# Four accumulator banks shared between two users, and a new order of units, in an attention and bilinear-FFN kernel

## Chip, cores, metric

One core of a Trainium2 chip. The metric is the device time of one execution in microseconds (us), the median of several; the profiled span is about 1.5 to 2 us shorter.

Engines: PE is TensorE (matmuls), DVE is VectorE, ACT is ScalarE, POOL is GpSimd (here it issues the loads), SP is SyncE (it issues the stores).

## The reference

```python
# 8 batches, 8 heads, 576 positions, 64 per head, 32 memory slots
a = softmax(phi, over positions)
k_m, v_m = einsum('bhsm,bhsd->bhmd', a, k), einsum('bhsm,bhsd->bhmd', a, v)
attn = softmax(q @ k_m.T / 8) @ v_m          # (b,h,s,d)
x = attn as 4608 rows of 512
out = ((x @ w_a) * (x @ w_b)) @ w_out        # d_ff = 1536
```

The kernel never forms `x`. It folds `v_m` into `w_a` and `w_b` for each batch ("fold", `pva`, result `vab`), then multiplies the attention weights by the folded matrices ("up": `pa`, `pb`; their product is `ht`), then by `w_out` ("down": `po`, 12 matmuls for 128 rows of the result).

## The kernel before

A batch's attention is cut into units: exponentials (`exp`), sums over positions (`kv`, `pkv`), transposes (`kvt`, `qt`), scores (`sc`), denominators (`dn`, `pD`, then two reciprocals `rD`), normalise (`nr`, `pR`) and six folds (`va`). The order in which they are emitted is the order on every engine.

```python
    ps_up = tile_pool(bufs=2, PSUM)     # two names, pa and pb: four banks
    ps_dn = tile_pool(bufs=2, PSUM)     # po
    ps_at = tile_pool(bufs=2, PSUM)     # everything of attention, tag "at"
    ...
        def denominators():
            pD = ps_at.tile([P, HALF], F32, name="pD", tag="at")
            ... four matmuls into pD ...
            for z in range(2):
                nc.vector.reciprocal(out=t["rD"][:, sl], in_=pD[:, sl])
        def fold(n, z):
            pvas = [ps_at.tile([P, 512], F32, name="pva", tag="at") for _ in range(2)]
            ... eight matmuls, alternating between the two ...
            nc.scalar.copy(out=vabs[b][z][:, 0, sl], in_=pvas[0])
            nc.vector.tensor_copy(out=vabs[b][z][:, 1, sl], in_=pvas[1])
    ...
    # ups(steps, side, rate): up steps of two slots each; side units spread evenly
    # over the slots; rate downs per step. run(b, names): units with nothing beside.
    run(0, "exp0 exp1 kv0 kv1 kvt qt0 qt1 sc0 sc1 dn va0a va0b nr0 nr1")
    ups(steps(0, 0, 4))
    load(2)
    run(1, "exp0 exp1 kv0 kv1 kvt qt0 qt1 va0a va0b sc0 sc1")
    run(0, "va1a va1b")
    run(1, "dn")
    ups(steps(0, 4, 6), named(1, "- - nr0 nr1"))
    ups(steps(1, 0, 4) + steps(0, 6, 8), named(1, "va1a va1b"))
    run(0, "va2a va2b")
    ups(steps(1, 4, 8) + steps(0, 8, 12), ...)
    load(3)
    ups(steps(1, 8, 12), ..., 5.2)
    run(2, "dn va1a va1b nr0 nr1 va2a va2b")
    for b in range(2, B):
        ups(steps(b, 0, NFF), named(b + 1, every), 5.2)
```

Loads are issued in the order batch 0, a third of `w_a` and `w_b`, batch 1, the rest of the weights.

The softmax here doesn't subtract the row's maximum and nothing guards it: scores larger than these inputs give would overflow.

## Time and profile before

| | before |
|---|---|
| time, median of 4 runs (range) | 302.44 us (301.09 to 302.77) |
| span of the profiled run | 301.0 us |
| PE, DVE, ACT busy | 258.1, 185.2, 127.9 us |
| mean granted PE clock | 0.966 |
| first up matmul | 28.24 us |
| batch 2's ups start, downs done by then | 96.11 us, 20 |

"Busy" adds up durations of matmuls that overlap, so 86% busy does not mean that 14% could be won.

### The profile page before, as it was taken

What the parts mean: (1) busy time and instruction counts of PE and PEld (TensorE: products, weight loads), DVE (VectorE), ACT (ScalarE), POOL (GpSimd) and SP (SyncE); (2) the same over time, 40 slices, a digit from 0 to 9 for tenths busy, and PEclk for the clock granted to TensorE, in tenths of its full rate; (3) what the DMA queues carried; (4) which work ended last, traced back from release to release, by engine and by line L of the source; (5) the groups of instructions that cost most, each with busy time, mean ns of one, the idle gap of its engine ahead of it and who ended that gap; (6) DMA issues with size and microseconds to landing.
All of it is one profiled execution on the core that took longest, in us unless ns stands there. A gap on an engine that the chain in (4) does not pass through costs nothing.

```text
span 301.0 us, 6648 instructions
## 1 busy us (share of the span) xinstructions
PE 258.1 (86%) x2640; PEld 137.8 (46%) x2640; DVE 185.2 (62%) x382; ACT 127.9 (43%) x307; POOL 32.8 (11%) x53
## 2 busy tenths in 40 slices
PE   0255848879957999999999999899999999999993
PEld 0122514546522554455445554455445544566541
DVE  5055556777865485866678576758677567745410
ACT  3022434566443346352644446444644354433400
POOL 8522221001200120002000200000000000000000
PEclk9999975999995899999999999999999999999999
DMA  6999999991970399228930594122111111212234
GB/s 145 203 246 207 206 207 248 246 181 29 195 130 2 85 164 180 48 55 173 208 70 12 148 206 100 38 57 50 38 35 35 39 39 34 65 40 58 50 79 96
DMA packets 24367, 33.46 MB, mean 111 GB/s; under 512 B 1808, under 2 KB 18704, under 8 KB 24336
## 3 DMA queue, kind: packets, MB, share of 16 engines
q0 software_dynamic: 18576, 23.60, 42.9%
q1 hardware_dynamic: 5760, 9.44, 12.8%
q8 instruction: 20, 0.33, 0.4%
q14 instruction: 11, 0.09, 0.1%
HBM read 42.47 MB, written 9.44 MB: 172 GB/s over the span
## 4 chain that ended last, share of the span: by engine, by line
PE 81%; DVE 9%; DMA 3%; ACT 3%; issue 1%; POOL 1%; DVEq 0%; POOLq 0%
PE po L279 30%; PE pa L328 17%; PE pb L337 17%; PE pva L243 7%; DVE rD L222 4%; DMA kv_sb<-in_v_dram 3%; PE pkv L157 3%; PE pscore L199 3%; ACT vab L251 2%; PE pR L229 2%; DVE qT L148 1%; DVE A L231 1%; PE pT L178 1%; PE pD L216 1%; DVE ht L340 1%
## 5 line engine op out<-in xcount | busy, mean ns | idle before, releaser
L279 PE MATMUL po<-wo_sb,ht 128*128 128x512 f16 x432 | 118.0, 382 | 0.0
L340 DVE TENSOR_TENSOR ht<-a_sb,pb 128x288 f16<-128x288 f16 x192 | 78.4, 448 | 58.1 <-PE pb L337 51.2
L331 ACT CAST a_sb<-pa 128x288 f16<-128x288 f32 x192 | 68.0, 405 | 74.7 <-PE pa L328 73.6
L328 PE MATMUL pa<-A,vab 128*128 128x288 f16 x384 | 66.5, 295 | 0.9 <-DVE A L231 0.8
L337 PE MATMUL pb<-A,vab 128*128 128x288 f16 x384 | 65.6, 292 | 0.1
L279 PEld LDWEIGHTS <-ht 128*128 128x128 f16 x432 | 42.6, 99 | 24.4 <-issue 0.6
L251 ACT CAST vab<-pva 128x512 f16<-128x512 f32 x48 | 28.1, 585 | 50.0 <-PE pva L243 50.0
L337 PEld LDWEIGHTS <-vab 128*128 128x128 f16 x384 | 36.8, 100 | 25.7 <-issue 5.5
L328 PEld LDWEIGHTS <-vab 128*128 128x128 f16 x384 | 33.9, 100 | 24.1 <-issue 10.2
L252 DVE CAST vab<-pva 128x512 f16<-128x512 f32 x48 | 33.0, 688 | 17.1 <-PE pva L243 17.0
L243 PEld LDWEIGHTS <-kvT 64*32 64x32 f16 x384 | 7.4, 90 | 36.7 <-issue 26.1
L208 ACT ACTIVATE E<-pscore,rphi 128x288 f16<-128x288 f32 x32 | 14.3, 497 | 20.6 <-PE pscore L199 20.6
L148 DVE STREAM_TRANSPOSE qT<-q_sb 128x576 f16<-128x576 f16 x32 | 22.6, 748 | 0.0
L243 PE MATMUL pva<-wb_sb,kvT 64*32 64x512 f16 x192 | 14.2, 421 | 9.1 <-ACT vab L251 4.2
L157 PE MATMUL pkv<-kv_sb,exp_sb 64*32 64x192 f16 x576 | 9.6, 259 | 14.1 <-DMA kv_sb<-in_v_dram 13.2
L285 DVE TENSOR_SCALAR o_sb<-po 128x512 f32<-128x512 f32 x18 | 12.3, 683 | 14.9 <-PE po L279 14.9
L287 ACT ACTIVATE o_sb<-po 128x512 f32<-128x512 f32 x18 | 10.8, 599 | 16.9 <-PE po L279 16.8
L222 DVE RECIPROCAL rD<-pD 128x144 f16<-128x144 f32 x16 | 15.7, 1026 | 3.3 <-PE pD L216 3.2
L243 PE MATMUL pva<-wa_sb,kvT 64*32 64x512 f16 x192 | 12.6, 413 | 5.3 <-DVE rD L222 3.3
L231 DVE SCALAR_TENSOR_TENSOR A<-E,rphi,pR 128x288 f16<-128x288 f16 x32 | 14.9, 510 | 3.3 <-PE pR L229 2.6
L79 POOL DMA_DIRECT2D phi_sb<-in_phi_dram x8 | 6.2, 776 | 92.6 <-ACT exp_sb L138 64.8
L157 PEld LDWEIGHTS <-exp_sb 64*32 64x32 f16 x576 | 6.4, 96 | 19.2 <-issue 16.2
(33 smaller groups left out, 92.9 us busy)
## 6 DMA issues: line engine op xcount, KB each, us to landing
out_dram<-o_sb SPq DMA_DIRECT2D x72, 128.0 KB, 2.4
phi_sb<-in_phi_dram POOLq DMA_DIRECT2D x8, 576.0 KB, 5.3
kv_sb<-in_k_dram POOLq DMA_DIRECT2D x8, 576.0 KB, 7.7
kv_sb<-in_v_dram POOLq DMA_DIRECT2D x8, 576.0 KB, 9.8
q_sb<-in_q_dram POOLq DMA_DIRECT2D x8, 576.0 KB, 10.4
wa_sb<-in_moe_w_a_dram POOLq DMA_DIRECT2D x3, 512.0 KB, 19.8
wb_sb<-in_moe_w_b_dram POOLq DMA_DIRECT2D x3, 512.0 KB, 19.8
wo_sb<-in_moe_w_out_dram POOLq DMA_DIRECT2D x3, 512.0 KB, 20.7
```

What stands on the lines that cost most here:

```text
L148: nc.vector.transpose(out=t["qT"][:, hp, :], in_=qs[b][:, hp, :])
L157: nc.tensor.matmul(t["pkv"][g][32 * j:32 * j + 32, :], t["exp"][64 * r:64 * r + 64, hp, i, :], kvs[b][64 * r:64 * r + 64, :, hp, D * i:D * ...
L222: nc.vector.reciprocal(out=t["rD"][:, sl], in_=pD[:, sl])
L231: nc.vector.scalar_tensor_tensor(out=attn[b][:, g, sl], in0=t["E"][:, g, sl], scalar=t["rphi"][:, g:g + 1], in1=pR, op0=ALU.mult, op1=ALU. ...
L243: nc.tensor.matmul(pvas[g][32 * j:32 * j + 32, :], t["kvT"][64 * r:64 * r + 64, 4 + g, M * j:M * j + M], w_sbs[z][64 * r:64 * r + 64, hp, sl],
L251: nc.scalar.copy(out=vabs[b][z][:, 0, sl], in_=pvas[0])
L252: nc.vector.tensor_copy(out=vabs[b][z][:, 1, sl], in_=pvas[1])
L279: nc.tensor.matmul(po, ht[:, i, P * c:P * (c + 1)], wo_sb[:, i, :], start=(i == 0), stop=(i == NFF - 1))
L328: nc.tensor.matmul(pa, vab[0][:, g, fs], A[:, g, HALF * hf:HALF * (hf + 1)], start=(g == 0), stop=(g == 1))
L331: nc.scalar.copy(out=a_sb, in_=pa)
L337: nc.tensor.matmul(pb, vab[1][:, g, fs], A[:, g, HALF * hf:HALF * (hf + 1)], start=(g == 0), stop=(g == 1))
L340: nc.vector.tensor_tensor(out=ht[:, i, t0:t0 + HALF], in0=a_sbs[hf], in1=pb, op=ALU.mult)
```

## The change

The intent: let down and attention draw from one pool of four banks, each time the one unused for longest; give each up slot at most one unit of attention, with downs in every slot; run batch 0 alone up to its last up step, so that batch 1's loads can come last; keep the array clock up with products of zeros while the first inputs arrive. All evictions of the result go to ScalarE. `...` marks cuts, some runs of lines are abridged, and most comments are mine.

```diff
-    ps_dn = ...tile_pool(name="ps_dn", bufs=2, PSUM)
-    ps_at = ...tile_pool(name="ps_at", bufs=2, PSUM)
+    ps_any = ...tile_pool(name="ps_any", bufs=1, PSUM)      # tags bank0..bank3
...
+    class Banks:
+        def take(self, shape, dtype, name, hold=False):
+            n = next(x for x in self.order if x not in self.held)
+            self.order.remove(n); self.order.append(n)
+            if hold: self.held.add(n)
+            return ps_any.tile(shape, dtype, name=name, tag=f"bank{n}"), n
+        def free(self, n):        # to the end of the order
...
+    def fill(n, cols=512):
+        for _ in range(n):
+            pw = ps_up.tile([P, 512], F32, name="pw", tag="pa")
+            nc.tensor.matmul(pw[:, :cols], warm[:, :P], warm[:, :cols], start=True, stop=True)
...
-    load(0); load_wab(0); ...; load(1); load_wab(1); load_wab(2); load_wo x3
+    load(0)      # phi on SP's queue; then k, q in halves, v
+    load_wab(0, 256); load_wab(256, 512); load_wab(512, 1024); load_wab(1024, 1536)
+    load_wo x3; load(1)
...
-        def denominators():        # pD, both reciprocals
+        def denominators(z):       # z=0: pD held, first reciprocal; z=1: let go, second
...
-        if cidx % 2:
+        if cidx % 2 and False:     # every o_sb on ScalarE
...
-    run(0, ...) ... run(2, "dn va1a va1b nr0 nr1 va2a va2b")
+    fill(16)
+    run(0, "exp0 exp1 ks")               # sums of k and of ones; v's follow later
+    fill(2); run(0, "kt qt0 qt1 qt2 qt3"); fill(3); run(0, "sc0"); fill(3)
+    run(0, "sc1 vs"); run(0, "vt dn0 dn1 vh0a vh0b"); fill(4); run(0, "nr0 nr1 nr2 nr3")
+    ups(steps(0, 0, 2), named(0, "- vh1a - vh1b"))
+    ups(steps(0, 2, 4), named(0, "- va1a - va1b"))
+    load(2)
+    ups(steps(0, 4, 8), named(0, "- va2a - va2b"))
+    ups(steps(0, 8, 12))
+    work.advance(24)                     # 24 downs
+    run(1, "exp0 exp1 ks"); work.advance(4)
+    ... batch 1's attention, 2 to 4 downs between its units ...
+    ups(steps(1, 0, 4), ...); ups(steps(1, 4, 12), <half of batch 2's attention>)
+    for x in "va0a dn0 va0b dn1 va1a nr0 nr1 va1b nr2 va2a nr3 va2b".split():
+        run(2, x); work.advance(2)
     for b in range(2, B):
-        ups(steps(b, 0, NFF), named(b + 1, every), 5.2)       # per step
+        ups(steps(b, 0, NFF), named(b + 1, every), 2.25)      # per slot, one unit a slot
```

## The prediction

> **What bounds the kernel now.** I read the page first (busy shares, then the span in forty slices), then TensorE's timeline in a steady stretch and around the holes, then its waits, then the issues of the load queue.
>
> TensorE (PE) is busy 86% of 301.0 us. The slices say where it isn't; each is 7.5 us, and the rows are PE, granted clock and DMA.
>
> ```profile
> PE   0255848879957999999999999899999999999993
> PEclk9999975999995899999999999999999999999999
> DMA  6999999991970399228930594122111111212234
> ```
>
> From slice 14 (about 98 us) PE is full. Before it there are holes, and two of them have a lowered clock. DMA is full to about 60 us. So the kernel has a start that waits, and a long body bound by PE.
>
> How good is the body? PE busy time can't tell, since matmuls overlap; I take distances from start to start.
>
> ```profile
> 201.07 0.66 PE L328 MATMUL pa<-A,vab 128*128 128x288 f16 x4
> 201.58 0.81 PE L279 MATMUL po<-wo_sb,ht 128*128 128x512 f16 x3
> 202.22 0.65 PE L337 MATMUL pb<-A,vab 128*128 128x288 f16 x4
> 202.71 0.59 PE L279 MATMUL po<-wo_sb,ht 128*128 128x512 f16 x2
> 203.24 0.53 PE L157 MATMUL pkv<-kv_sb,exp_sb 64*32 64x192 f16 x32
> 203.69 0.66 PE L328 MATMUL pa<-A,vab 128*128 128x288 f16 x4
> ```
>
> Four up matmuls take 0.49 us, a down matmul 0.216 (three in 0.65). The same view gives the attention units of a batch, up to the start of the next matmul: sums 0.62+0.55, transposes 0.67, six folds of 0.425 = 2.55, scores 2x0.46, denominators 0.34, normalise 2x0.25; 6.15 us in all. The whole program is 192 up halves x 0.49 = 94.1, 432 downs x 0.2163 = 93.4, 8 x 6.15 = 49.2: 236.7 us. The last matmul ends at 283.38+60x0.2163 = 296.4, 4.7 before the end. A PE that never waited would need 241.4; about 60 us are lost.
>
> Where? Almost all in the first 100 us. Two places: batch 2's attention, run with nothing beside it,
>
> ```profile
> 86.65 0.31 PE L216 MATMUL pD<-E,sel 128*32 128x288 f16 x4 [0.69 <-ACT vab L251]
> 86.89 0.39 PE L243 MATMUL pva<-wa_sb,kvT 64*32 64x512 f16 x1
> 89.03 0.41 PE L243 MATMUL pva<-wa_sb,kvT 64*32 64x512 f16 x7 [1.76 <-DVE rD L222]
> 90.13 0.77 PE L243 MATMUL pva<-wb_sb,kvT 64*32 64x512 f16 x8 [0.69 <-ACT vab L251]
> ...
> 96.11 1.14 PE L328 MATMUL pa<-A,vab 128*128 128x288 f16 x4
> 97.04 1.49 PE L279 MATMUL po<-wo_sb,ht 128*128 128x512 f16 x3
> ```
>
> and the loads. In PE's waits:
>
> ```profile
> PE pkv L157 <- DMA kv_sb<-in_v_dram: 13.2, 1, 13.2
> PE pva L243 <- DVE rD L222: 6.4, 7, 1.8
> PE pva L243 <- ACT vab L251: 4.9, 7, 0.7
> ```
>
> In the second hole each fold waits for a bank that VectorE's reciprocals (2x1.0 us) or an eviction still holds: attention has two banks. The rD wait comes seven times, once per later batch. In the steady batches it stops PE about 1.2 us: reciprocals are 32.6 us apart on average, against 11.76+62.4x0.2163+6.15 = 31.4 of work (rate 5.2 a step gives 62.4 downs).
>
> The load queue (POOL) issues in order, and each late issue waits for an earlier landing, which dates the landings:
>
> ```profile
> 13.34 0.74 POOL L88 DMA_DIRECT2D wa_sb<-in_moe_w_a_dram  x1 [2.10 <-DMA kv_sb<-in_v_dram]
> 16.18 0.74 POOL L89 DMA_DIRECT2D wb_sb<-in_moe_w_b_dram  x1 [2.09 <-DMA q_sb<-in_q_dram]
> 18.73 0.74 POOL L88 DMA_DIRECT2D wa_sb<-in_moe_w_a_dram  x1 [1.82 <-DMA wa_sb<-in_moe_w_a_dram]
> 49.27 0.74 POOL L84 DMA_DIRECT2D q_sb<-in_q_dram  x1 [2.07 <-DMA wo_sb<-in_moe_w_out_dram]
> ```
>
> An input of one batch takes 2.85 us, a third of w_a 2.55; batch 0, batch 1 and all weights are in by 49.2 us.
>
> **What the Trainium skill says.** "TensorE: Matmul & The Clock Gate", Part 1, says that the array's clock is halved after an idle window of about 3.4 us and restored after as long a busy one. This trace agrees: after the hole at 86 to 96 four up matmuls take 0.93 us (96.11 to 97.04), and 0.49 from 100.2 on. That is what zero products can prevent. "TensorEngine Tiling (Array Packing)", Key Properties, says a change of tiling mode drains PE. Here it is small: downs at 202.71 would be through at 203.14, the sums start at 203.24. "PSUM — Partial Sum Buffer", Specifications, gives 8 banks. Both kernels use eight (pa 2, pb 2, then 2+2 before and 4 shared after), so only who may take which changes. "DMA: Bandwidth & Descriptors", Specifications, puts the ceiling of 16 engines at 435 GB/s; an input of 1.18 MB (fp32, by shape) in 2.85 us is 414, so loads can be reordered, not sped up.
>
> **The change part by part.**
>
> *Batch 0.* Its phi goes out on SP's queue and k is the first load on POOL's, so the chain of landings is some 0.7 us earlier (an issue takes 0.74 to 0.89). Order: k, q, v, w pieces, w_out, batch 1. At the measured pace: k 9.5, q 12.5, v 15.4, the first quarters of w_a, w_b 16.7 and 18.0, then 20.6, 25.7, 30.8 for the later w_b pieces, w_out 38.5, batch 1's k 43, q 46, v 49. Zero products (28 of them, at most 0.43 us each at the halved clock) lie almost wholly inside these waits. Attention then needs, after v: sums 1, copies and transposes 1.5, then VectorE's two reciprocals 2.0 and normalise 3x0.5. The first up product comes at about 22.3, against 28.24 before. Batch 0's twelve steps run alone at 1.13 us or, with a fold, 1.5 (VectorE 0.82+0.69): done at about 38.
>
> *Batch 1.* 24 downs (5.2 us) to 43.3, then its attention with 18 downs between. It is bound by the loads: v at 49, sums and transposes to 52.3, VectorE reciprocals and two fold copies 3.4, normalise 1.5: first up product at about 57.3. Its steps and the first half of batch 2's attention: 11.76 + four folds 1.7 + 2.76 = 16.2, plus 2.0 because VectorE has 17 us of work there. To 75.5.
>
> *Batch 2's second half* now has 24 downs between its units: 5.2+2.55+0.34+0.5 = 8.6, plus 1 of waits: batch 2's ups start at 85.1 with 66 downs done. Before: 96.1 with 20 downs done. That is 11.0 us earlier with 46x0.2163 = 10.0 us more done: a gain of 21.
>
> *The body.* Remaining: 366 downs 79.2, 72 steps 70.6, five attentions 30.75, and 4.7 at the end: 185.2. Before it was 412 downs, 195.2 in sum, and took 204.9: 9.7 of waits and slow clock (five rD waits of 1.2, about 1.9 of halved clock after 96, rest scattered). With four banks, least recently used, folds no longer take the bank that reciprocals hold: pD is marked held until the second is issued, a fold takes two others, last used two slots (2.5 us) earlier. Rate 2.25 a slot is 54 downs a batch, exactly what a batch brings, but 66 had been done of 108: in batches 2 and 3 downs run out for the last five and three slots, where VectorE (2.0 us per two slots against PE's 1.5) binds: 2 us. Five steady batches at 0.4 and 0.5 for the lone steps at the end: 4.5 instead of 9.7, a gain of 5.
>
> *Evictions.* All o_sb go to ScalarE: 18x0.599 = 10.8 us more there, 12.3 less on VectorE. Steady ScalarE load becomes some 17 of 30 us, VectorE 21. Neither binds; it relieves the fuller one.
>
> Sum: 85.1+185.2+4.5 = 274.8 us of span, 26 less. Runs are 1.5 above the span (302.48 against 301.0): 276.3.
>
> **The rivals.**
> 1. *The loads eat the gain.* Batch 0 alone means batch 1 is loaded last; if v of batch 1 landed at 55 rather than 49 (w quarters in short rows, output writes beside them), all after it moves as much: 282. For it: the DMA row is full to 60 us. Against: the same bytes landed by 49.2 before.
> 2. *Shared banks make new waits.* A held down plus held sums leave one free bank; po's eviction now queues behind ScalarE's other work. At 1.2 us a batch as before: 280; at 2, 285. Against: four buffers rotate where two did, and steady ScalarE has 40% idle.
> 3. *The clock stays high throughout and chains are shorter than I sum*: batch 1's PE work is done early and only the load binds: 270.
> 4. *Nothing gained* (302) would need new waits of 26 us. Nothing in the profile points to it.
>
> **Range and chances.** The start's estimates add up four chains, each good to 2 us; bank waits 0 to 1.2 us times six batches, that is up to 7; the clock 2. I take 276 with 270 to 283. A gain under 2% would need 296 or more, 20 us off; slower is nearly out of the question.
>
> **What would show it.** First pa matmul near 22 us, batch 1's near 57, batch 2's near 85. PE's slices full from about slice 8, except a dip at 44 to 57 with its wait on v of batch 1. The rD wait of folds gone; steady reciprocals about 30 us apart. Downs at the tail still 60. Wrong: if the fold still waits for rD or o_sb each batch, if batch 1's v lands after 53, or if a lowered clock shows beyond 60 us.

## The result, and the profile after

The changed kernel takes 274.24 us (273.63 to 275.22, four runs) against 302.44 us. The ratio is 0.9078, with a 95% interval of 0.9036 to 0.912. Ratios here and below are the mean time of one kernel's fast runs over that of the other's fast runs of the same rounds, so not quite the ratio of the medians quoted. The result is correct against the reference.

The page of the changed kernel: span and busy time, then the slices (6.8 us each) of PE, its granted clock and DMA.

```profile
span 271.9 us, 7025 instructions
PE   7578997889999999999999999999999999999992
PEclk9899999999999999999999999999999999999999
DMA  7999999999991695159714991211111111112253
```

PE's row is at 9 from 61 us on (8 in the slice before), where it was from about 98 us, and no slice shows a half clock. The zero products count as busy in the first slice.

PE's timeline of the changed kernel at the three points that the prediction named: batch 0's first ups, batch 1's, batch 2's.

```profile
21.09 0.28 PE L394 MATMUL pa<-A,vab 128*128 128x288 f16 x1 [0.24 <-DVE A L287]
...
56.51 0.28 PE L394 MATMUL pa<-A,vab 128*128 128x288 f16 x1
57.23 0.71 PE L394 MATMUL pa<-A,vab 128*128 128x288 f16 x3 [0.44 <-DVE A L287]
...
84.41 0.65 PE L394 MATMUL pa<-A,vab 128*128 128x288 f16 x4
```

The first matmuls stand at 21.1, 56.5 (the next three at 57.2) and 84.4 us, where 22.3, 57.3 and 85.1 were predicted.

PE's waits in the body, first the kernel before from 96.2 us to the end, then the changed kernel from 84.4 us:

```profile
PE pva L243 <- DVE rD L222: 3.1, 5, 0.9
PE pR L229 <- DVE A L231: 0.6, 1, 0.6
```

```profile
PE pva L298 <- ACT o_sb L353: 0.3, 2, 0.2
```

The wait of a fold for the bank that reciprocals read, once a batch, is gone; two of 0.2 us for an eviction have come. From 84.41 to the end are 187.5 us for 185.2 of work.

The chain of waits of the changed kernel between 15 and 52 us (start, duration, what):

```profile
15.52 15.27 DMA wb_sb<-in_moe_w_b_dram
...
37.74 5.20 PE po L344 x24
...
42.96 0.60 ACT o_sb L353
43.55 1.15 ACT exp_sb L181 x2
...
44.75 0.77 PE pkv L203 x68
...
50.98 0.75 PE pkv L203 x72
```

The last piece of `w_b` lands at 30.8, as estimated, and the ups run to 37.6. Then come 24 downs, and here is something the prediction lacks: the exponentials of batch 1 begin only when the second result has been evicted, since they were issued to ScalarE after it, and PE waits for them. The issue of k of batch 1 at 23.44 lands 19.6 us later, at 43.0, and v's, at 31.08, 19.2 later, at 50.3.

### The profile page after: what moved, and what is told of

Same layout as the page of the kernel before. It is cut to its first block, busy times and chain, and to the rows that moved or that the text cites. A ratio compares the mean times of both kernels' runs of the same rounds, so it can differ in the third digit from the quotient of the medians.

```text
span 271.9 us, 7025 instructions
## 1 busy us (share of the span) xinstructions
PE 254.7 (94%) x2828; PEld 135.5 (50%) x2828; DVE 170.6 (63%) x369; ACT 136.3 (50%) x331; POOL 34.9 (13%) x56
## 4 chain that ended last, share of the span: by engine, by line
PE 80%; DMA 10%; DVE 4%; ACT 2%; issue 1%; POOL 1%; ACTq 0%; DVEq 0%; POOLq 0%
PE po L344 34%; PE pa L394 17%; PE pb L403 17%; DMA wb_sb<-in_moe_w_b_dram 6%; PE pva L298 5%; DMA kv_sb<-in_v_dram 4%; PE pkv L203 3%; PE pscore L253 2%; PE pR L285 1%; DVE qT L190 1%; DVE ht L406 1%; ACT o_sb L353 1%; PE pT L232 1%; DVE rD L278 1%; PE pT L238 1%
## 5 line engine op out<-in xcount | busy, mean ns | idle before, releaser
L394 PE MATMUL pa<-A,vab 128*128 128x288 f16 x384 | 64.1, 287 | 1.3 <-DVE A L287 1.2
L403 PE MATMUL pb<-A,vab 128*128 128x288 f16 x384 | 64.0, 286 | 0.6 <-DVE ht L406 0.3
L308 ACT CAST vab<-pva 128x512 f16<-128x512 f32 (+1 forms) x54 | 29.5, 554 | 35.6 <-PE pva L298 35.5
L403 PEld LDWEIGHTS <-vab 128*128 128x128 f16 x384 | 36.0, 98 | 22.2 <-issue 2.2
L394 PEld LDWEIGHTS <-vab 128*128 128x128 f16 x384 | 32.8, 97 | 26.3 <-issue 13.3
L353 ACT ACTIVATE o_sb<-po 128x512 f32<-128x512 f32 x36 | 21.7, 602 | 30.5 <-PE po L344 30.5
L310 DVE CAST vab<-pva 128x512 f16<-128x512 f32 x46 | 31.4, 683 | 4.5 <-PE pva L298 3.9
L218 DVE CAST kvm<-pkv 128x128 f16<-128x128 f32 (+1 forms) x20 | 4.9, 256 | 24.9 <-PE pkv L203 24.9
L203 PE MATMUL pkv<-kv_sb,exp_sb 64*32 64x192 f16 (+2 forms) x720 | 10.2, 230 | 4.9 <-DMA kv_sb<-in_k_dram 3.3
L181 ACT ACTIVATE exp_sb<-phi_sb 128x576 f16<-128x576 f32 x16 | 10.9, 694 | 2.6 <-DMA phi_sb<-in_phi_dram 2.6
L298 PE MATMUL pva<-wb_sb,kvT 64*32 64x512 f16 (+1 forms) x200 | 10.5, 378 | 1.6 <-DVE rD L278 0.9
```

The lines of the kernel that those rows point to most:

```text
L203: nc.tensor.matmul(t[key][g][0][32 * j:32 * j + 32], t["exp"][64 * r:64 * r + 64, hp, i, :], kvs[b][64 * r:64 * r + 64, part, hp, D * i:D ...
L298: nc.tensor.matmul(pvas[g][32 * j:32 * j + 32, 0:hi - lo], t["kvT"][64 * r:64 * r + 64, 4 + g, M * j:M * j + M], w_sbs[z][64 * r:64 * r + ...
L308: nc.scalar.copy(out=vabs[b][z][:, g, lo:hi], in_=pvas[g][:, 0:hi - lo])
L310: nc.vector.tensor_copy(out=vabs[b][z][:, g, lo:hi], in_=pvas[g][:, 0:hi - lo])
L353: nc.scalar.mul(out=o_sb, in_=po, mul=1.0 / (CS * CS))
L394: nc.tensor.matmul(pa, vab[0][:, g, fs], A[:, g, HALF * hf:HALF * (hf + 1)], start=(g == 0), stop=(g == 1))
```

## The experiments

Twelve runs were made, in three calls, each call on one chip (the first and the third on the same one) with its own runs of the kernel before and of the changed kernel as control. All were correct.

| run | median us | ratio to before | 95% interval |
|---|---|---|---|
| control, first call | 276.07 | 0.9146 | 0.911 to 0.9182 |
| no zero products | 275.47 | 0.9136 | 0.9102 to 0.9171 |
| shared banks, pD let go | 277.52 | 0.9191 | 0.9158 to 0.9224 |
| two and two banks | 291.62 | 0.9671 | 0.9632 to 0.9709 |
| control, second call | 276.13 | 0.9132 | 0.9093 to 0.9171 |
| exponentials between downs | 273.77 | 0.9046 | 0.9011 to 0.9082 |
| batch 1's denominators first | 273.95 | 0.9047 | 0.9005 to 0.909 |
| kernel before with shared banks | 286.81 | 0.9466 | 0.9423 to 0.951 |
| control, third call | 276.22 | 0.9159 | 0.9115 to 0.9203 |
| kernel before, downs in the hole | 296.05 | 0.9812 | 0.9781 to 0.9844 |
| evictions alternate | 276.57 | 0.9169 | 0.9134 to 0.9204 |
| batch 1 reordered, no zero products | 271.87 | 0.9013 | 0.8985 to 0.9042 |

**The controls** (`e0`, `e4`, `e8`: no edit).

> The changed kernel again, unaltered, so that the variants of this call have a control on the same chip. Expected: 273.6 to 275.2 us, as its four runs gave; ratio to before 0.905 to 0.912.

> The changed kernel unaltered, as control for this call, since the ratio moved from 0.908 to 0.915 between two sessions. Expected 273.5 to 276.5 us.

> The changed kernel unaltered, control for this call: 274 to 277 us, ratio to before 0.908 to 0.915.

They agree with each other to 0.3% and lie about 2 us above the four runs of the result; the first missed its expectation by 0.9 us. One kernel's profiled runs differ by as much: the first up matmul stood at 21.09 us in the profile of the result and at 23.66 in that of the first control, where v landed later and four zero products ran at half clock. So differences under 1 us in the medians are not read below, and only runs of one call are compared closely. The scatter arises at the front: from batch 2's denominators to the start of the last downs the profiles of the result, of all three controls, of the run without zero products and of two with a new order for batch 1 (exponentials between downs, denominators first) take 176.92 us each. A difference in this stretch can be read far more finely than one in the medians.

**No zero products.**

```diff
-        for _ in range(n):
+        for _ in range(0):
```

> All 28 zero products taken out. Theory (clock): the array runs at half clock through batch 0's attention and its first ups, so the first up product comes 1 to 2 us later, and the ups of steps 0 to 3 take longer; since the chain of batch 0 meets w_b's last piece at 30.8 us with only some 0.2 us to spare, 1 to 2.5 us are added to the whole. Rival A (absorbed): batch 0's steps wait for the weights anyway and batch 1's v lands at 50.3, so the time is the same within 0.5 us. Rival B (the zero products delay: four of them stand between the reciprocals and normalise): 0.5 to 1 us faster.

0.9136 against 0.9146: no difference. The timeline of that run:

```profile
9.58 1.16 PE L203 MATMUL pkv<-kv_sb,exp_sb 64*32 64x128 f16 x72 [9.58 <-DMA kv_sb<-in_k_dram]
...
20.83 0.43 PE L394 MATMUL pa<-A,vab 128*128 128x288 f16 x1
...
22.36 1.16 PE L403 MATMUL pb<-A,vab 128*128 128x288 f16 x4
```

The array does run slower: the sums last 1.16 us where the changed kernel's last 0.80, and the first four pb take 1.09 to the next start instead of 0.58. But the first up product comes no later, because its chain waits for loads, transposes and reciprocals, and the ups then meet the weights' landing. The theory of the clock falls, and "absorbed" holds: the zero products are worth nothing here. The rival that they delay is true where they stand: from batch 0's denominators to its first up product are 3.9 us in both runs without them, and 4.4 to 5.6 in all profiles of the new order with them (7.2 with split banks). The ups' wait for the weights hides that too. A warning on reading: the granted clock reads 1.00 from 9 to 26 us in this run, while the four pb at 22.36 take 1.09 us. Here the slow rate has to be read from the matmuls.

**Shared banks with pD let go, and two banks for each.** The first issues both reciprocals in one unit and doesn't hold pD's bank; the second adds a split:

```diff
-            if z == 1:
-                banks.free(t["bank"])
-            ... one reciprocal ...
+            if z == 1:
+                return
+            banks.free(t["bank"])
+            for y in range(2): ... both reciprocals ...
```

```diff
-            n = next(x for x in self.order if x not in self.held)
+            n = next(x for x in self.order if x not in self.held and (x < 2) == (name == "po"))
```

(With two banks for attention pD can't be held over a fold: its two tiles would both need the one bank left, and its matmuls alternate between them. Hence the first as the split's own control.)

> Four shared banks kept, but both reciprocals are issued in one slot and the bank of pD is not held over the fold. Theory (the four banks in rotation keep folds off pD's bank, holding is a detail): same as control within 0.7 us. Rival (the hold and the reciprocals apart are what removes the wait): the rD wait of about 1 us a batch comes back, 4 to 7 us slower.

> As the run with pD let go, but down takes only banks 0 and 1 and attention only 2 and 3, as in the kernel before. Theory: folds wait for pD's bank again, 0.7 to 1.2 us in each of seven batches, and the folds of batch 1 and 2 that stand close together wait for evictions: 5 to 10 us slower than control, with PE's wait of pva on rD back at about 0.5 to 0.9 us seven times. Rival (the order with one unit a slot and downs between spaces folds far enough apart): under 2 us slower; then the sharing of banks is worth little and the order is what counts.

Letting pD go gives 277.52 against 276.07. The intervals overlap, so the time alone is unclear. The profile settles it. PE's waits with pD let go:

```profile
PE pva L300 <- DVE rD L280: 3.5, 4, 1.4
PE po L346 <- DVE rD L280: 0.9, 1, 0.9
```

The control has one such wait, of 1.1 us: the oldest bank is now and then pD's. From batch 2's denominators to the last downs this run takes 179.52 us instead of 176.92 (77.61 to 257.13). The hold, with the reciprocals apart, is worth 2.6 us in that stretch: more than the theory's 0.7, less than the rival's 4 to 7.

The split costs 14 us more, 15.55 against the control, past the top of the expected 5 to 10. PE's waits with two and two banks, and its timeline in a steady batch:

```profile
PE pva L300 <- DVE rD L280: 7.6, 8, 1.5
```

```profile
201.92 0.39 PE L300 MATMUL pva<-wa_sb,kvT 64*32 64x512 f16 x1
203.03 0.41 PE L300 MATMUL pva<-wa_sb,kvT 64*32 64x512 f16 x7 [0.71 <-DVE rD L280]
```

The first fold matmul goes to the free bank, the second waits 1.1 us for pD's. The denominators' matmuls (pD) mark each batch in PE's timeline, and show where the time goes, in us (the profiled run of the split was the fastest of its six, so the sum is 12.5 and not 14):

| batch | shared, pD let go | two and two | behind by |
|---|---|---|---|
| 0 | 16.99 | 16.96 | 0 |
| 1 | 53.65 | 55.42 | 1.8 |
| 2 | 77.61 | 82.42 | 4.8 |
| 3 | 102.02 | 110.30 | 8.3 |
| 7 | 219.90 | 231.51 | 11.6 |
| last downs start | 257.13 | 269.60 | 12.5 |

Eight of the 12.5 us arise before batch 3's denominators, where units of batches 1 and 2 stand close together, and where PE also runs at half clock for a while (four downs from 85.23 to 86.88 us, 1.65 us instead of 0.87). Only some 4 arise in the steady batches. Whether attention needs to share with down, or only to have more than two banks (three and one, say), was not run.

**The kernel before with shared banks.** Its order and loads as they were; every tile of `ps_at` and `ps_dn` from the shared pool, po and the sums held:

```diff
-    ps_dn = ...; ps_at = ...
+    ps_any = ...; class Banks as above
-            pvas = [ps_at.tile([P, 512], F32, name="pva", tag="at") for _ in range(2)]
+            pvas = [banks.tile([P, 512], F32, name="pva") for _ in range(2)]
  ... the same for pT, pscore, pD, pR; pkv and po with hold=True and free ...
```

> The kernel before, its order and loads untouched, only with down and attention taking four banks least recently used (down and the sums hold theirs). With the run of two and two banks in the new order this makes a square: order old or new, banks split or shared. Theory (the two parts act on different waits and add): 10 to 13 us faster than before, as sharing is worth in the new order. Rival (the old order, with two units close together and no downs in batch 2's attention, keeps most waits whatever the banks): 3 to 7 us faster.

286.81 against 302.85: 16 us, more than both expected. The square in ratios to the kernel before:

| | two and two banks | shared |
|---|---|---|
| old order and loads | 1 | 0.9466 |
| new order and loads | 0.9671 | 0.9191 (pD let go) |

5.3% and 3.3% alone; 8.1% together. The two parts nearly add, and sharing is the larger. "New order and loads" stands for all the rest of the change, pieces, zero products and evictions on ScalarE included; the order of the loads was not run alone. Sharing's gain in the old order again begins early: against the kernel before, batch 1's denominators are 6.3 us earlier (42.08 against 48.36), batch 2's 8.1, batch 3's 10.0; the five steady batches after add 5.1 us to the start of the last downs.

**The kernel before, with downs in the hole.**

```diff
-    run(2, "dn va1a va1b nr0 nr1 va2a va2b")
+    for x in "dn va1a va1b nr0 nr1 va2a va2b".split():
+        run(2, x)
+        work.advance(4)
```

> The kernel before with one thing: four downs after each of the seven units of batch 2's attention that it runs with nothing beside it (28 downs, 6.1 us of TensorE work). Theory (that hole of about 11.6 us, with 6.2 us of work in it and the half clock after it, is a large part of what the new order gains): 5 to 8 us faster than before, and the up matmuls after the hole at 0.49 us for four from the start. Rival (with two banks for attention the units wait as long as before and the downs only lengthen the stretch; or TensorE has to wait later for want of downs): under 3 us faster.

```profile
86.10 1.04 PE L279 MATMUL po<-wo_sb,ht 128*128 128x512 f16 x4
...
88.24 0.41 PE L243 MATMUL pva<-wa_sb,kvT 64*32 64x512 f16 x7 [0.79 <-DVE rD L222]
...
95.78 0.65 PE L328 MATMUL pa<-A,vab 128*128 128x288 f16 x4
```

The ups start at 95.8 where they did at 96.1, so the stretch is as long as before, but 28 downs are done in it: 28x0.2163 = 6.1 us. What comes out is 6.1 between the medians, 5.7 by the ratio. The ups after it run at 0.49 us for four from the first. This one line is over half of the 10 us that the whole new order gains with banks split.

**Exponentials between downs.**

```diff
-    work.advance(24)
-    run(1, "exp0 exp1 ks")
+    work.advance(12)
+    run(1, "exp0 exp1")
+    work.advance(12)
+    run(1, "ks")
```

> Batch 1's two exponentials are issued after 12 of the 24 downs, not after all: ScalarE runs them between the two evictions, so the sums start when k lands. Theory of the chain of waits (downs, then exponentials, then sums bind batch 1): the 1.6 us that PE waits for exp_sb go, and all after is 1.3 to 1.6 us earlier. Rival, the recorded prediction's reason (the load of batch 1's v binds, landing at 50.3 when the sums of v start at 50.9): at most 0.6 us faster.

273.77 against 276.13, and the intervals of the ratios don't touch. ScalarE's timeline of this run, then PE's:

```profile
42.87 0.60 ACT L353 ACTIVATE o_sb<-po 128x512 f32<-128x512 f32 x1 [2.69 <-PE po L344]
43.37 1.25 ACT L181 ACTIVATE exp_sb<-phi_sb 128x576 f16<-128x576 f32 x2
```

```profile
40.09 5.34 PE L344 MATMUL po<-wo_sb,ht 128*128 128x512 f16 x24
45.36 0.80 PE L203 MATMUL pkv<-kv_sb,exp_sb 64*32 64x128 f16 x72
```

The sums follow the downs at once. From batch 0's first up product to batch 1's denominators are 30.1 us (22.98 to 53.08) against 31.9 in the control (21.49 to 53.40), so 1.8 of the 2.4 us are the chain. So the chain of waits was right: in the profiles of the result and of the controls batch 1 was bound by PE's and ScalarE's own order, not by v's landing. The rest is not explained. In the control's profile batch 1's first ups ran at half clock and lost 1.5 us, from denominators to denominators of batches 1 and 2 (25.3 us against 23.8 here); but the other two controls show 23.8 too, so this was one profile's mishap.

**Batch 1's denominators first, and the last version.** Both have the exponentials between downs. The first moves `dn0` ahead of `vs` and `dn1` right after it; the second also puts two downs after each of batch 1's folds and drops the zero products:

```diff
     run(1, "sc1")
-    work.advance(2)
-    run(1, "vs")
-    work.advance(2)
-    run(1, "vt dn0")
-    ... va0a dn1, va0b nr0 nr1 nr2 nr3 ...
+    work.advance(4)
+    run(1, "dn0 vs dn1")
+    work.advance(2)
+    run(1, "vt")
+    work.advance(2)
+    run(1, "va0a")
+    work.advance(2)          # only in the last version
+    run(1, "va0b")
+    work.advance(2)          # only in the last version
+    run(1, "nr0 nr2 nr1 nr3")
```

> A version meant to be better: exponentials between downs as in the run before, and batch 1's denominators and first reciprocal ahead of the sums of v, the second right after them, so that VectorE's 2 us of reciprocals run while v lands; normalise in the order that the first up product needs. Theory: the first up product of batch 1 comes 2 to 3 us earlier, time 1.5 to 3 us less than control. Rival (v's landing plus its chain of sums, copies, transposes and folds bind): under 1 us.

> A version meant to beat both: the exponentials of batch 1 between downs, its denominators ahead of the sums of v, two downs after each of its two folds in place of the idle stretch that halved the clock in the run before, and no zero products. Theory: the 2.4 us of the exponentials plus about 1 for the clock and the four zero products ahead of batch 0's normalise: 2.5 to 4 us faster than control, ratio to before 0.899 to 0.905. Rival (v's landing bounds batch 1 and eats the rest): the 2.4 us only, ratio 0.905 to 0.907.

The first gave nothing over the exponentials alone (0.9047 and 0.9046). Its profile shows what became of the earlier start: batch 1's ups start whole at 57.08 us, but at half clock, 1.29 us for the first four, so that pb follows at 58.37, where it came at 58.42 with the exponentials alone. The last version is the fastest of all: 271.87 us, 0.9013, with an interval apart from its control's, 4.4 us in the medians. PE's timeline in it:

```profile
49.53 0.37 PE L272 MATMUL pD<-E,sel 128*32 128x288 f16 x4
50.14 0.75 PE L203 MATMUL pkv<-kv_sb,exp_sb 64*32 64x64 f16 x72 [0.25 <-DMA kv_sb<-in_v_dram]
...
55.58 1.44 PE L394 MATMUL pa<-A,vab 128*128 128x288 f16 x4
```

Now PE does wait for v (0.25 us), and the ups begin at 55.6 with 46 downs done instead of 42. Of batch 1's ups one group still ran at half clock. This run has several edits at once; how much each gives beyond the exponentials is not told apart.

**Evictions alternate again.**

```diff
-        if cidx % 2 and False:
+        if cidx % 2:
```

> The changed kernel with every second o_sb evicted by VectorE again (18 of 0.683 us there, 18 of 0.6 us fewer on ScalarE). Theory (neither engine binds the body): within 1 us of control. Rival (VectorE is the fuller one in batch 1's and 2's steps and where downs run out, its queue delays the products): 1.5 to 3 us slower.

276.57 against 276.22: the same. But that is the sum of two opposite effects. A row of PE's timeline, then one of its waits:

```profile
43.44 0.80 PE L203 MATMUL pkv<-kv_sb,exp_sb 64*32 64x128 f16 x72
...
PE pva L298 <- DVE o_sb L351: 2.1, 2, 1.1
```

With the second eviction on VectorE, batch 1's exponentials no longer stand behind it, and the sums follow the downs at once (43.44 us). From batch 0's first up product to batch 1's denominators are 29.3 us (21.82 to 51.16) against 31.2 in this call's control (22.04 to 53.25): again the 1.8 to 1.9 us that the exponentials between downs gave, by another edit. From batch 2's denominators to the last downs it is 179.79 us instead of 176.92, and folds wait for VectorE's evictions. So the move to ScalarE is worth 2.9 us in the body and costs 1.9 at the front. The theory's number came true, its reason didn't.

## Why the prediction was right, and where its reasons were not

The time, 274.24 us, lies in the range of 270 to 283 and 1.8 us under the 276 that the prediction took; the controls' 276.1 to 276.2 lie on it. No large errors cancel in the sum of the span: batch 2's ups came 0.7 us early, and the body had 2.2 us less of waits. Point by point:

- *Landings.* Right: the last piece of `w_b` 30.8 (predicted 30.8), k of batch 1 43.0 (43), v 50.3 (49). Reading the pace of loads off the queue's waits was enough.
- *Batch 0's first ups.* 21.1 us against 22.3, and 21.5 to 23.7 in the controls.
- *"It is bound by the loads: v at 49"*, of batch 1. The time was nearly right (56.5 against 57.3), the reason was not, so the agreement is partly luck. What bound it was the weights, the ups, 24 downs, and the exponentials behind an eviction; v came 0.6 us ahead of need, and 1.8 to 2.6 in the controls' profiles. The exponentials between downs show it, with 2.4 us gained although v landed at 49.7 us against 49.9 in the control; had v bound it, that edit would have given a few tenths. The alternating evictions show it a second time. What failed was to sum each engine's work without asking in which order ScalarE would get it.
- *The front's 21 us.* Measured 11.7 us earlier (84.41 against 96.11) and 46 downs more done, 10.0 us: 21.7 in all. The step counted this as the gain of the order. The runs put much of it to the banks: sharing them in the old order brings batch 2's denominators 8.1 us forward, and splitting them in the new one puts batch 3's 8.3 us back. I had named the two banks as what the folds of the old hole waited for, but worked out the new front with chains almost free of bank waits (1 us), so the banks' gain was in the sum and credited to the order.
- *The body's gain of 5.* Mis-sized: the waits left are 2.3 us, not 4.5, against 9.7 before, so 7.4 were gained. The 2 us for slots without downs do not show: there PE's two slots take 1.55 us from start to start (109.02 to 110.57), its own work. That VectorE makes up its lag afterwards is likely, but no run tests it. In the old body, "five rD waits of 1.2" are 0.9 to 1.25 each, from the fold's first matmul to its second, and the seven rD waits of the whole are those of batches 0 and 2 to 7, not one per later batch.
- *Zero products.* The prediction said that they lie inside waits, and gave them no gain; but it also called the half clock what they "can prevent". They did not: in the first control, with them, the clock is 0.50 from 20 to 24 us. The last four do not lie in a wait but ahead of the normalise. Without them nothing is lost.
- *The clock.* The idle window of 3.4 us that the prediction quotes is not what the trace shows: in the old hole PE's longest unbroken wait is 1.8 us, and the clock is down from about 90 us on. No run tests what brings it down.
- *Loads.* The 414 GB/s count bytes read from HBM. Written as fp16 they are half, and the trace's own row, which counts these, stands at 200 to 210 from 10 to 18 us in the kernel before. That the loads cannot be sped up was not tested. The DMA row is at 9 to 68 us, not to 60.
- *The hold of pD*, which the prediction made the reason why folds no longer wait, is worth 2.6 us. The larger part, 14 us, is four banks instead of two and two.
- *Evictions.* "Neither binds; it relieves the fuller one" was half right: the relief gave 2.9 us in the body, but the eviction ahead of batch 1's exponentials took back 1.9.
- *Signs.* Downs at the tail are 63, not 60; steady denominators are 27.7 to 30.3 us apart.
- *Rivals.* Loads did not eat the gain; no new wait over 0.3 us came in the body; the third (chains shorter, 270) was nearest to the miss, and the last version, at 271.9, shows its room.

The section "Matmuls" of the Trainium skill's "Perfetto Trace Analysis" says that independent groups of matmuls should rotate through different banks, so that one's evacuation overlaps the next. The runs agree: the same eight banks, with four in one rotation instead of two and two, make 16 us of 302.85 in the old order and 14 in the new.

## What to carry to other kernels

Before banks are dealt out to users for good, look for the user that waits for an eviction while another's bank stands idle; one pool in order of last use took 5% off here, with no other change. Fill stretches of dependent small units with independent large matmuls: 28 downs in a 10 us stretch did not lengthen it. And when an engine takes work in issue order, an early input is of no use if its first instruction stands behind an eviction that waits for PE: follow each engine's order, not only its load. When an edit "changes nothing", compare stretches of the two profiles before believing it: two effects of 2 and 3 us cancelled here.

## What the Trainium skill lacked or had wrong

- "PSUM — Partial Sum Buffer": it gives the number of banks and says to evacuate promptly, but nothing on sharing banks between users of different pace. Here 2+2 against 4 shared is 302.85 against 286.81 us, and 291.62 against 277.52 us.
- "TensorE: Matmul & The Clock Gate", Part 1: its advice to keep the array busy holds for the rate of matmuls (four ups in 0.49 against 0.93 us), but it does not say that a slow array costs nothing where a chain of other engines bounds the stretch: 28 zero products removed, 275.47 against 276.07 us, with the sums at 1.16 us instead of 0.80.
- "TensorEngine Tiling (Array Packing)", Key Properties: it gives no size for the drain at a change of mode. Between 512-column matmuls and the tiled sums about 0.1 us shows (203.14 to 203.24 us in the kernel before).
- "DMA: Bandwidth & Descriptors", Bandwidth: its table does not say how a load that casts counts. Here loads from fp32 to fp16 ran at 414 GB/s counted in HBM bytes and half that counted in SBUF bytes (1.18 MB read in 2.85 us); the profile's GB/s row, near 200 in that stretch, counts the latter.
